# Three query tiles of an attention and gated-convolution kernel cast before they are turned, turned by the DMA engines instead of TensorE, under a newly searched order

## The chip, the core and the metric

The kernel runs on one core of a Trainium2 chip. The metric is the device time of the program in microseconds (us), as the median of several runs. Before the change it is 183.54 us (three runs, 183.1 to 183.88). One execution was taken by the hardware profiler; all durations below are from that one.

## What is computed

Inputs are q, k, v of 4 batches x 8 heads x 768 positions x 64 channels and three weight arrays. Attention keeps, for each query, the 6 best of 24 chunks of 32 keys; the rank of a chunk is an upper bound of its scores, made from the smallest and the largest key of the chunk in each channel. The result goes through a gated unit whose gate is a causal convolution of 5 taps.

```python
k_min, k_max = k_chunks.min(axis=3), k_chunks.max(axis=3)        # 24 chunks of 32 keys
ub = np.sum(np.maximum(q * k_min, q * k_max), axis=-1)           # query x chunk, causal chunks only
top_chunks = np.argsort(ub, axis=-1)[..., -6:]
scores = np.where(selected & causal, (q @ k.T) / 8, -1e9)
attn_out = softmax(scores) @ v                                   # B, H, S, 64 -> x: B, S, 512
gate = sigmoid(causal_conv5(x, conv_w))
out = (gate * (x @ w_val)) @ w_out
```

## The kernel before, in words

The 32 heads are worked on as 16 pairs (p = 0 to 15), two heads side by side on the 128 partitions; four pairs make one batch b. Every operation has a name, and the table ORDER (line 114) lists all names in the order in which they are emitted. Each engine carries out its own operations strictly in that order, each one waiting by semaphores for what it needs. So an operation whose input is late holds up all that stands behind it on its engine. The number behind "=" in ORDER is the PSUM bank that the operation takes.

For one pair (function pair in build, lines 297 to 480):

- Lk, Lq, Lv load k, q, v (line 632 for k and q, 628 for v), issued by SyncE (SP). Pair 0 is loaded in two parts, Lq0.0 and Lq0.1.
- KT and QT turn k and q on TensorE (PE), in fp32, 3 blocks of 128x128 to each of two halves w (line 641). KE (ScalarE, line 648) takes k out of PSUM as fp16; KX (VectorE, line 654) takes the smallest and largest key of each chunk. QH (ScalarE, line 683) gives the high fp16 part of 16 q, and QL (VectorE, line 722) the rest that fp16 lost, for the 640 queries from 128 on.
- KB, KS (GpSimd, lines 664 to 679) make the sums and differences of the chunk ends; AH and AL (VectorE, lines 729 and 732) the absolute values RH, RL of the two parts of q.
- CF and BD (PE, line 766; for pair 0 instead BF, line 714, in fp32) sum the upper bounds in PSUM. T8 (VectorE, line 774) finds the 8 largest, CM (line 781) writes the mask NS. The mask is turned either by PE and VectorE (MT, line 791, and ME, line 795) or, for pairs 10 to 15, by a DMA transpose that SP issues (MD, line 797).
- S (PE, lines 809, 811, 814): for each of six score banks the products of keys and queries, and the mask added by a second matmul (line 814). E (ScalarE, line 818): exp of a bank into P, for each of the two heads. A (GpSimd, line 830): the causal triangle. AV (PE, line 839), RC and NR (VectorE, lines 845 and 849): the sum over values and its division.
- XT turns the result for the second part: by PE and VectorE (XT, line 871, and XTE, line 882), or for pairs 8 to 14 by a DMA transpose (line 863). XH (GpSimd) copies 4 columns across block edges.

For two pairs, CV (PE, line 903) is the convolution, 160 small matmuls in two halves CVp.0 and CVp.1, and TH (ScalarE, line 908) its tanh. For each batch VL (PE, line 918, 16 matmuls) makes x w_val, GV (VectorE, line 924) the gate's product, OU (PE, line 932) the last product, OE (ScalarE, line 940; a few on VectorE, 942) takes it out, ST (SP, line 945) stores it. In the last batch VL is in two halves, VL3.n and VL3.nz.

At the start PE runs 36 matmuls on zeros, F and G (line 950), between the first operations. All loads of k, q and v, all stores and all DMA transposes go through SP's one queue. There is no planner at run time.

## Time and profile before

| | before |
|---|---|
| runs | 183.1, 183.54, 183.88 us |
| the profiled execution | 182.86 us |
| its span, first to last instruction | 181.2 us |
| busy: TensorE, its weight loads | 175.2, 127.3 us |
| busy: ScalarE, VectorE, GpSimd | 140.4, 123.3, 109.1 us |
| granted TensorE clock, mean | 1.00 |

The profiled execution's own time is 182.86 us, of which 181.2 lie between its first and its last instruction. Busy times count an instruction from its start to its end. Matmuls overlap, so a PE that is busy 97% of the span may still have been waiting between issues; the chain of waits and the start times of single pieces tell more. In a timeline row stand the start in us, the duration in us, engine, line and operation, what it writes and reads, the number of instructions merged, and in brackets the idle time of the engine ahead of it.

### The profile page before, as it was taken

The page shows a single profiled execution, that of the slowest core. Times are in us where ns is not written, and L with a number is a line of the kernel's source. Part 1 is how long each engine was busy: PE and PEld are TensorE (multiplying, and loading weights), DVE is VectorE, ACT ScalarE, POOL GpSimd, SP SyncE. Part 2 cuts the span into 40 slices and gives each one's busy share as a digit, 9 for nine tenths or more (in the row PEclk, how much of TensorE's full clock was granted, in tenths as well). Part 3 has the DMA queues.
Part 4 walks back from the last instruction along what each step waited for, and adds up shares of the span by engine and source line. Part 5 has one row for each costly group of instructions (what it writes and reads, how often), then busy time and mean ns, then how long its engine had stood idle before and what let it go on. Part 6 is the DMA issues. An engine that isn't in the chain of part 4 may idle for free.

```text
span 181.2 us, 8892 instructions
## 1 busy us (share of the span) xinstructions
PE 175.2 (97%) x3714; PEld 127.3 (70%) x3714; DVE 123.3 (68%) x429; ACT 140.4 (78%) x320; POOL 109.1 (60%) x309
## 2 busy tenths in 40 slices
PE   7999999999999999999999999999999999999991
PEld 5896667868878687787866685687567678656541
DVE  0569999999999799998765679558925233611360
ACT  2279999999999999999897867595867979357032
POOL 6955898999999979899919633374551615000000
PEclk9999999999999999999999999999999999999999
DMA  5999999999999999980697995895226149337045
GB/s 99 224 220 215 213 201 236 213 211 227 210 222 190 219 191 189 183 175 10 135 164 150 207 206 117 176 95 149 43 47 103 60 117 231 96 108 289 7 183 222
DMA packets 89912, 29.68 MB, mean 164 GB/s; under 512 B 85387, under 2 KB 86667, under 8 KB 89872
## 3 DMA queue, kind: packets, MB, share of 16 engines
q1 hardware_dynamic: 88880, 28.06, 73.5%
q0 software_dynamic: 992, 1.06, 4.5%
q8 instruction: 29, 0.48, 1.2%
q14 instruction: 11, 0.09, 0.2%
HBM read 20.98 MB, written 6.29 MB: 151 GB/s over the span
## 4 chain that ended last, share of the span: by engine, by line
PE 91%; DVE 5%; issue 1%; POOL 0%; ACT 0%
PE ps L918 12%; PE ps L839 12%; PE ps L932 12%; PE ps L641 11%; PE ps L811 10%; PE ps L903 9%; PE ps L814 9%; PE ps L766 6%; PE ps L950 4%; DVE KK L654 2%; PE ps L871 2%; PE ps L791 2%; PE ps L809 2%; PE ps L714 1%; DVE ON L849 1%
## 5 line engine op out<-in xcount | busy, mean ns | idle before, releaser
L818 ACT ACTIVATE P<-ps 128x512 f16<-128x512 f32 (+1 forms) x192 | 90.2, 600 | 5.4 <-PE ps L814 4.8
L830 POOL TENSOR_SCALAR_AFFINE_SELECT P<-P 128x256 f16<-128x256 f16 (+1 forms) x128 | 43.1, 358 | 23.6 <-ACT P L818 21.9
L654 DVE TENSOR_REDUCE KK<-ps 128x12 f32<-128x384 f32 x64 | 32.8, 550 | 7.1 <-PE ps L641 6.5
L814 PE MATMUL ps<-QM,EM 64*128 64x512 f16 (+4 forms) x256 | 36.9, 290 | 0.2
L811 PE MATMUL ps<-QH,KE 64*128 64x512 f16 (+4 forms) x256 | 35.1, 291 | 0.0
L924 DVE SCALAR_TENSOR_TENSOR GV<-G,ps 128x384 f16<-128x384 f32 x32 | 16.4, 548 | 22.8 <-PE ps L918 22.1
L839 PEld LDWEIGHTS <-P 128*128 128x128 f16 x672 | 26.1, 98 | 6.3 <-issue 3.3
L839 PE MATMUL ps<-VA,P 128*128 128x65 f16 x672 | 30.3, 194 | 0.2 <-issue 0.2
L940 ACT ACTIVATE OSB<-ps 128x512 f32<-128x512 f32 (+1 forms) x22 | 12.9, 594 | 15.6 <-PE ps L932 8.4
L918 PE MATMUL ps<-xT,wv 64*128 64x384 f16 x256 | 23.3, 323 | 0.3 <-issue 0.3
L932 PE MATMUL ps<-wo,GV 128*128 128x512 f16 (+1 forms) x100 | 22.7, 370 | 0.0
L774 DVE MAX8 TOP<-ps 128x8 f32<-128x16 f32 (+4 forms) x160 | 15.9, 166 | 6.6 <-PE ps L766 5.1
L918 PEld LDWEIGHTS <-wv 64*128 64x128 f16 x256 | 13.1, 94 | 8.3 <-issue 1.2
L908 ACT ACTIVATE G<-ps 128x384 f32<-128x384 f32 x32 | 13.9, 498 | 6.6 <-PE ps L903 6.6
L811 PEld LDWEIGHTS <-KE 64*128 64x128 f16 x256 | 13.6, 94 | 6.2 <-issue 1.6
L849 DVE TENSOR_TENSOR ON<-ps,RCP 128x384 f16<-128x384 f32 x32 | 17.5, 552 | 0.7
L648 ACT ACTIVATE KE<-ps 128x384 f16<-128x384 f32 x32 | 17.0, 569 | 1.0 <-DVE RCP L845 0.7
L683 ACT ACTIVATE QH<-ps 128x384 f16<-128x384 f32 x32 | 16.0, 556 | 2.3 <-PE ps L641 2.2
L903 PE MATMUL ps<-xT,diag 32*32 32x384 f16 x1280 | 17.3, 326 | 0.0
L741 POOL CAST VA<-vn 128x768 f16<-128x768 f32 x16 | 14.6, 915 | 3.8 <-DMA vn<-in_v_dram 3.7
L641 PE MATMUL ps<-ident,kn 128*128 128x128 f32 x96 | 15.7, 284 | 0.0
L903 PEld LDWEIGHTS <-diag 32*32 32x32 f16 x1280 | 14.0, 87 | 2.5 <-ACT P L818 0.4
(75 smaller groups left out, 304.3 us busy)
## 6 DMA issues: line engine op xcount, KB each, us to landing
vn<-in_v_dram SPq DMA_DIRECT2D x16, 384.0 KB, 6.1
out_dram<-OSB SPq DMA_DIRECT2D x23, 256.0 KB, 2.9
kn<-in_k_dram SPq DMA_DIRECT2D x30, 192.0 KB, 5.0
qn<-in_q_dram SPq DMA_DIRECT2D x30, 192.0 KB, 4.8
wv<-in_moe_w_val_dram POOLq DMA_DIRECT2D x8, 64.0 KB, 4.5
wo<-in_moe_w_out_dram POOLq DMA_DIRECT2D x4, 128.0 KB, 5.3
wv<-wv SPq DMA_DIRECT2D x4, 128.0 KB, 5.1
qn<-in_q_dram SPq DMA_DIRECT2D x4, 96.0 KB, 3.1
```

The lines of the kernel that those rows point to most:

```text
L641: nc.tensor.transpose(out=pt[:, tl * 128:(tl + 1) * 128], in_=t[:, 3 * w + tl, :], identity=ident)
L648: nc.scalar.activation(out=KE[p % 3][:, w * HB:(w + 1) * HB], in_=bank(gr, None), func=AF.Copy)
L654: nc.vector.tensor_reduce(out=KK[p % 2][:, mx, w * 12:(w + 1) * 12], in_=bank(gr, None).rearrange("p (c t) -> p c t", t=CH), axis=AX.X, op ...
L811: nc.tensor.matmul(out=pq[hh][:, col + a:col + n], lhsT=KE[p % 3][HP[hh], ks], rhs=QH[p % 3][HP[hh], q0 + a:q0 + n], start=True, stop=False)
L814: nc.tensor.matmul(out=pq[hh][:, col + a:col + n], lhsT=EM[HP[hh], ks], rhs=qm[HP[hh], q0 + a - 128:q0 + n - 128], start=False, stop=True)
L818: e.EX = lambda p, hh, bi, tot, gr: nc.scalar.activation(out=PT[hh, bi, p % 2][:, 0:tot], in_=bank(gr, None)[:, 0:tot], func=AF.Exp, scale ...
L830: nc.gpsimd.affine_select(out=ap, in_=ap, pattern=[[0, n], [1, 128]], compare_op=ALU.is_ge, fill=0.0, base=0, channel_multiplier=-1)
L839: nc.tensor.matmul(out=pav[:, qt, :], lhsT=PT[a, bi, p % 2][:, col:col + 128], rhs=VA[p % 3][:, hh, jt, :], start=(jt == 0), stop=(jt == qt))
L849: e.NR = lambda p, hh, gr: nc.vector.tensor_tensor(out=ON[(p // 2) % 2][:, 2 * (p % 2) + hh].rearrange("p t h d -> p h t d"), in0=bank(gr, ...
L903: nc.tensor.matmul(out=pc[i][os], lhsT=diag[rs, cp * NG + gi, j, :], rhs=x[rs, gi, :, a:a + 128], start=(j == 0), stop=(j == 2 * KSZ - 1), ...
L918: nc.tensor.matmul(out=pv[h], lhsT=wval_sb[HP[h], n, wc:wc + 255:2], rhs=xT[HP[h], (b % 2) * 2 + cp, gi, :, LD:LD + 128], start=(n == 0), ...
L932: nc.tensor.matmul(out=po[:, 0:z - a], lhsT=GVT[(b % 2) * NCT + et][:, s * 128:(s + 1) * 128], rhs=wout_sb[:, et, a:z], start=(et == 0), s ...
```

## The change

For pairs 13, 14 and 15 the operations QT, QH and QL go. In their place QN.0 (ScalarE) casts the 768 loaded, unturned queries to the high fp16 part, QN.1 (VectorE) makes the low part of 640 of them, and two DMA transposes on SP, QD.0 and QD.1, write them turned into QH and QL. The fp16 buffer of QN shares one tile (CW, two halves by p % 2) with the convolution's weights, which are loaded at the start. All else of the computation stays. The whole of ORDER is another one; the operations are the same but for the ones named.

```diff
+    "dmaq": set(range(13, 16)),
...
-        for w in range(2):
+        if p in P["dmaq"]:
+            b2 = p % 2
+            c, l = act(S)
+            g.op("ACT", c, l, f"QN{p}.0", lambda: e.QN(p, 0), [("qn", k4, 0), ("qn", k4, 1), ("cwps",)],
+                 [("QN", b2, 0)], ())
+            c, l = dve(SELT * 128)
+            g.op("DVE", c, l, f"QN{p}.1", lambda: e.QN(p, 1),
+                 [("qn", k4, 0), ("qn", k4, 1), ("QN", b2, 0)], [("QN", b2, 1)], ())
+            g.op("SP", 1300, 1300, f"QD{p}.0", lambda: e.QD(p, 0), [("QN", b2, 0)],
+                 [("QH", k3, w) for w in range(2)], (), dma=700.0)
+            g.op("SP", 1250, 1250, f"QD{p}.1", lambda: e.QD(p, 1), [("QN", b2, 1)],
+                 [("QL", k2, w) for w in range(2)], (), dma=650.0)
+        for w in range(2) if p not in P["dmaq"] else ():
...
-    cwl = ct_([KSZ, 2 * NG, 64], FP, "cwl")
-    cwn = ct_([KSZ, 2 * NG, 2, 64], FP, "cwn")
+    CW = ct_([128, 1536], FP, "CW")
...
+    QNA = CW.bitcast(F16).rearrange("p (i x) -> p i x", i=2)
...
+    def QN(p, n):
+        hi, lo = QNA[:, p % 2, 0:S], QNA[:, p % 2, S:S + SELT * 128]
+        t = qn[p % 4]
+        if n == 0:
+            nc.scalar.activation(out=hi, in_=t.rearrange("p t d -> p (t d)"), func=AF.Copy, scale=QS)
+        else:
+            nc.vector.scalar_tensor_tensor(
+                out=lo, in0=t[:, 1:NT].rearrange("p t d -> p (t d)"), scalar=QS, in1=hi[:, 128:S],
+                op0=ALU.mult, op1=ALU.subtract)
...
+    def QD(p, n):
+        dst, src = (QL[p % 2], QNA[:, p % 2, S:S + SELT * 128]) if n else (QH[p % 3], QNA[:, p % 2, 0:S])
+        nc.sync.dma_start_transpose(out=dst.rearrange("p (t c) -> p t c", c=128), in_=src)
...
 ORDER = """
-mKF0 wval30 mfz F0=0 F1 F2 F3 F4 F5 mxT F6 F7 F8 ident identb mKB1 cfill identh mVA0 F9 F10 F11 F12
...
+mfz F0=0 F1 F2 F3 F4 F5 F6 F7 F8 F9 F10 F11 F12 F13 F14 ident F15 Lk0.0 Lk0.1 mKF0 wval30 mxT identb
```

The order moves instructions on every engine. Three places follow, before and after. In the names, qn2 is the loaded q of pair 2, kn1 the loaded k of pair 1, ps_5 PSUM bank 5, fz the zeros of the F and G matmuls; "x3" are three instructions alike.

On PE, near the program's start, before: the transposes of pair 1's k (KT1) and of the second half of pair 0's q (QT0.1), one G matmul, and the first of the five bound sums of pair 0 (BF, lines 706 and 714).

```order
L641 MATMUL ps_5_261<-ident_61,kn1_75 128x128 x3
L641 MATMUL ps_6_267<-ident_61,kn1_75 128x128 x3
L641 MATMUL ps_7_279<-ident_61,qn0_78 128x128 x3
L950 LDWEIGHTS fz_145
L950 MATMUL ps_1_212<-fz_145 128x256
L706 LDWEIGHTS identb_65
L706 MATMUL ps_0_284<-cfill_64,identb_65 128x48
L714 MATMUL ps_0_284<-KF_105,QF_106 128x48 x2
```

The transposes of pair 2's q (QT2.1 and QT2.0) stand behind the fifth BF here.

The same place after the change, from QT0.1 (now line 655) to the first BF (now lines 720 and 728).

```order
L655 MATMUL ps_7_255<-ident_61,qn0_77 128x128 x3
L982 LDWEIGHTS fz_144
L982 MATMUL ps_1_221<-fz_144 128x256
L655 MATMUL ps_5_264<-ident_61,kn1_74 128x128 x3
...
L655 MATMUL ps_6_273<-ident_61,kn1_74 128x128 x3
...
L655 MATMUL ps_2_289<-ident_61,qn2_79 128x128 x3
L655 MATMUL ps_4_294<-ident_61,qn2_79 128x128 x3
L720 LDWEIGHTS identb_65
L720 MATMUL ps_0_299<-cfill_64,identb_65 128x48
L728 MATMUL ps_0_299<-KF_104,QF_105 128x48 x2
```

QT0.1 now stands ahead of both KT1, and both QT2 stand ahead of the five BF instead of behind them. Ahead of this piece 10 G matmuls stand in a row.

On VectorE, a little later, before: the end of the weights' split (cws), the mask of pair 0 taken out of PSUM (ME0, line 795) and what follows it.

```order
L1047 CAST cw2_71<-cwT_70 128x40
L1048 TENSOR_TENSOR cw2_71<-cwT_70,cw2_71 128x40
L795 COPY QM0_89<-ps_0_358 128x640
L722 SCALAR_TENSOR_TENSOR QL0_99<-ps_4_312,QH2_98 128x256
L722 SCALAR_TENSOR_TENSOR QL1_100<-ps_6_354,QH1_97 128x256
```

After the change, the same place.

```order
L1079 CAST cw2_70<-cwT_69 128x40
L1080 TENSOR_TENSOR cw2_70<-cwT_69,cw2_70 128x40
L743 TENSOR_SCALAR RH1_101<-QH1_96 128x640
L827 COPY QM0_88<-ps_0_365 128x640
L736 SCALAR_TENSOR_TENSOR QL0_98<-ps_4_294,QH2_97 128x256
```

AH1 (RH1, now line 743) has moved ahead of ME0.

On SP, in the second half, before: from the loads of pair 14 (kn2, qn2) to the mask transpose MD12 (QM0) and the next transposes and loads.

```order
L632 DMA kn2_76<-in_k_dram 128x6x64 x2
L632 DMA qn2_80<-in_q_dram 128x6x64 x2
L628 DMA vn0_82<-in_v_dram 128x12x64
L628 DMA vn3_85<-in_v_dram 128x12x64
L632 DMA kn3_77<-in_k_dram 128x6x64 x2
L632 DMA qn3_81<-in_q_dram 128x6x64 x2
L863 DMA_TRANSPOSE xT_73<-ON0_149 128x6x128
L945 DMA out_0_dram<-OSB3_170 128x512
L797 DMA_TRANSPOSE QM0_89<-NS0_119 128x5x128
```

After the change, the same stretch of SP's queue.

```order
L646 DMA kn2_75<-in_k_dram 128x6x64 x2
L764 DMA_TRANSPOSE QH1_96<-CW_68 128x6x128
L646 DMA qn2_79<-in_q_dram 128x6x64 x2
L642 DMA vn0_81<-in_v_dram 128x12x64
L646 DMA kn3_76<-in_k_dram 128x6x64 x2
L895 DMA_TRANSPOSE xT_72<-ON0_148 128x6x128
L764 DMA_TRANSPOSE QL1_99<-CW_68 128x5x128
L764 DMA_TRANSPOSE QH2_97<-CW_68 128x6x128
L829 DMA_TRANSPOSE QM0_88<-NS0_118 128x5x128
L764 DMA_TRANSPOSE QL0_98<-CW_68 128x5x128
L646 DMA qn3_80<-in_q_dram 128x6x64 x2
```

Four of the six QD (line 764) have come in between; pair 15's q is now loaded behind them and behind MD12 (line 829), and pair 15's v later still.

## The prediction

> **What bounds the kernel now.** I read the page first: the span, the busy times and the chain that ended last.

> ```profile
> span 181.2 us, 8892 instructions
> PE 175.2 (97%) x3714; PEld 127.3 (70%) x3714; DVE 123.3 (68%) x429; ACT 140.4 (78%) x320; POOL 109.1 (60%) x309
> PE 91%; DVE 5%; issue 1%; POOL 0%; ACT 0%
> ```

> The chain lies on PE for 91% of the span. But 78% for ACT is a mean over stages, so the busy times by stage come next (columns: PE, its weight loads, DVE, ACT, POOL, granted clock, DMA).

> ```profile
> 15.80:60.00 44.20, 43.78 (x787) 32.63 (x788) 42.92 (x162) 44.14 (x105) 39.09 (x110) 1.00 1.13 213
> 60.00:98.00 38.00, 37.72 (x1065) 29.24 (x1067) 32.33 (x110) 35.37 (x81) 30.75 (x84) 1.00 0.79 153
> 98.00:165.50 67.50, 67.50 (x1658) 47.15 (x1656) 34.75 (x115) 48.84 (x108) 27.30 (x84) 1.00 0.61 135
> 165.50:171.30 5.80, 5.48 (x69) 3.21 (x66) 1.57 (x3) 1.64 (x4) 0.00 (x0) 1.00 0.25 91
> ```

> The reader should see two regimes. From 15.8 to 60 us ACT works 44.14 of 44.20 us: the stage lasts as long as its exps and copies, from the first exp on. From 98 to 165.5 us PE works without a gap and ACT only 48.84 of 67.5. Between them both are nearly full (37.72 and 35.37 of 38). So work taken off PE after 98 us shortens the span at its full price, and a later first exp moves all that follows.

> **What goes.** The three changed pairs have their q transposes here, as merged pieces of the chain:

> ```profile
> 106.23 1.97 PE ps L641 x18
> 121.11 1.35 PE ps L641 x12
> ```

> The first piece holds QT13 and QT14 (12 transposes) beside KT14 (6), the second QT15 (6) beside KT15. One costs 1.97/18 = 0.109 us and 1.35/12 = 0.1125 us, so 12 x 0.109 + 6 x 0.1125 = 1.98 us of PE go, all where PE has no gap: **-1.98 us**.

> ACT and DVE give and take work in the same stage:

> ```profile
> L683 ACT ACTIVATE QH<-ps 128x384 f16<-128x384 f32 x32 | 16.0, 556 | 2.3 <-PE ps L641 2.2
> L722 DVE SCALAR_TENSOR_TENSOR QL<-ps,QH 128x256 f16<-128x256 f32 (+1 forms) x30 | 13.8, 480 | 0.7 <-ACT QH L683 0.4
> ```

> Six QH go (6 x 0.556 = 3.3 us); three QN.0 of 768 columns come, no row has that shape, and each costs between one QH and two (0.56 to 1.11). Six QL go (6 x 0.48 = 2.9 us); three QN.1 come, between one QL and two (0.48 to 0.96). Neither engine gets more work, and ACT has 67.5 - 48.84 = 18.7 us free there, DVE 32.75: nothing on the path. If that cover were gone the worst would be nothing still, since removed and added work are equal at the upper bounds.

> **What comes on SP.** Six DMA transposes, like those that are there:

> ```profile
> L797 SPq DMA_TRANSPOSE QM<-NS x6: 1201/1251/2170, 85.9 to 137.3; - x6
> DMA to landing us min/median/max: 2.5/2.6/3.5
> L863 SPq DMA_TRANSPOSE xT<-ON x7: 1242/1392/4467, 106.5 to 155.8; - x7
> DMA to landing us min/median/max: 2.7/3.6/7.5
> ```

> Each holds SP's queue 1.2 to 1.4 us and lands 2.6 to 3.6 us after issue; the slowest took 4.47 and 7.5. The place that counts is MD12, the mask transpose for which the first S12 waits on PE:

> ```profile
> 111.30 1.20 SPq L797 DMA_TRANSPOSE QM<-NS  x1
> 115.23 0.23 PE L811 MATMUL ps<-QH,KE 64*128 64x128 f16 x2
> ```

> Landing 2.6 us after 111.30 is 113.9; PE comes at 115.23, so 1.3 us are spare. Now QD13.1 and QD14.0 stand ahead of MD12 (2 x 1.25 = 2.5 us), but Lv15 and Lq15 have left that place, so SP arrives no later. I take 0 to 0.4 us for all new waits of this kind, **+0.2**, since the transposes nearest in kind (L797) spread little; the upper end is a rival. Behind QN13.0 and QN14.0 on ACT stand TH3 and the last E11, behind QN15.0 E12.10 and KE15; a wait there for a load falls into ACT's 18.7 free us. AL14 on DVE waits for QD14.1, and behind it stands GV1.2, whose bank PE needs only at VL1.0, three S12 later.

> **What is moved at the start.** Here the new order does something that has nothing to do with q's transposes. The chain to the first exp before:

> ```profile
> 8.77 0.82 PE L641 MATMUL ps<-ident,kn 128*128 128x128 f32 x6
> 9.63 0.52 PE L641 MATMUL ps<-ident,qn 128*128 128x128 f32 x3
> 10.13 0.62 PE L714 MATMUL ps<-KF,QF 128*128 128x48 f32 x4
> 12.54 0.84 PE L641 MATMUL ps<-ident,qn 128*128 128x128 f32 x6
> 12.74 0.92 DVE L774 MAX8 TOP<-ps 128x8 f32<-128x24 f32 x10 [1.50 <-PE ps L714]
> 14.81 0.49 DVE L795 COPY QM<-ps 128x640 f16<-128x640 f16 x1
> 15.80 1.08 ACT L818 ACTIVATE P<-ps 128x512 f16<-128x512 f32 x2 [0.16 <-PE ps L814]
> 16.81 0.32 DVE L729 TENSOR_SCALAR RH<-QH 128x640 uint16<-128x640 uint16 x1
> ```

> BF (L714) runs from 10.13 to 12.54, T8 waits for its end, and the mask (L795) and the first exp (15.80) follow. The loads that PE waits for, by issue on SP and time to landing:

> ```profile
> 5.88 0.49 SPq L632 DMA_DIRECT2D qn<-in_q_dram  x1
> qn<-in_q_dram SPq DMA_DIRECT2D x1, 96.0 KB, 3.6
> 6.94 0.89 SPq L632 DMA_DIRECT2D qn<-in_q_dram  x1
> qn<-in_q_dram SPq DMA_DIRECT2D x1, 192.0 KB, 4.3
> ```

> The second part of q0 lands at 5.88 + 3.6 = 9.5, q2 at 6.94 + 4.3 = 11.25. In SP's queue both keep their place (loads of the same sizes stand ahead). In the new order PE must do QT0.1, both KT1 and both QT2 before the first BF. QT0.1 starts at about 9.6, as before; KT1 and four zeros' matmuls follow until about 10.9 (the first piece's six took 0.82 for twice three, the zeros 0.11 each, by the piece quoted last); QT2 must wait for 11.25 plus the 0.15 us between landing and start that QT0.1 shows, and takes 6 x 0.11 = 0.66. BF starts at 12.05 instead of 10.13: 1.9 us later. AH1 now stands ahead of ME0 on DVE: 0.32 by the row at 16.81. The first exp comes 1.9 + 0.32 = 2.2 us later. ACT has the same operations before it (KE, QF, KF, QH of pairs 0 to 2) and can draw none forward, so the whole full stage of ACT moves: **+2.2 us**. Bounds: 0 if the loads land 2 us sooner, 2.6 if DVE's pieces stand less tightly. I take 2.2, since landings and order are both fixed.

> **Near the end** PE waits once in the last batch's VL:

> ```profile
> 98.21 1.30 PE ps L918 x16
> 165.54 3.03 PE ps L918 x36
> 168.57 0.32 issue
> 168.89 2.45 PE ps L918 x28
> ```

> Its 64 matmuls and the gap take 5.80 us; at 1.30 for 16 they would take 5.20. VL3.0 now comes first, in banks that CV13 and an OU leave, instead of VL3.1, which waits for TH15. I take **-0.4** of the possible 0.6 (0 if TH15 or GV3 is late in its place). CV13's two halves stand apart now. What an interruption costs is seen on CV3 and a whole one:

> ```profile
> 95.35 1.01 PE ps L903 x69
> 96.38 1.29 PE ps L903 x91
> 158.01 1.98 PE ps L903 x160
> ```

> 2.30 against 1.98: **+0.2**, between 0 and 0.3. The other switches between S and full-array work differ by a few and are not priced.

> **The sum** against the profiled execution's span: -1.98 + 0.2 + 2.2 - 0.4 + 0.2 = +0.2 us, from 181.2 to 181.4. That execution took 182.86 us in all, 1.7 outside its span; the median of the runs is 0.7 above it, and I add the sum to the median: 183.54 + 0.2 = 183.7 us. What a measurement of this kernel can tell from no change is about 0.5%, 0.92 us.

> [...] First the row:

> ```profile
> 1.22 4.88 PE ps L950 x22
> 7.73 1.20 PE ps L950 x11
> ```

> The same zeros' matmul takes 0.222 us at first and 0.109 later: PE ran at half rate until about 7 us, and never again in this trace. In the new order PE idles from about 8.4 (the end of its 10 G in a row, an estimate with 0.222 until 7 us and 0.11 after) to 9.6 and again 0.3 us before QT2, and from 8.4 to 12 us does little but transposes. [...]

> **The rivals.**

> *The late start costs nothing* (faster). If the loads land sooner, or the stage from 60 to 98 us takes up the delay (ACT is idle there 38 - 35.37 = 2.6 us), the 2.2 go: 183.7 - 2.2 = 181.5. For it: both engines are a little below full there. Against: PE is at 37.72 of 38, so ACT's idle time is waiting for PE, and a delay of both is not taken up. It decides if the first BF starts before 10.5 us. Chance 0.30.

> *MD12 is late* (slower). One of the two QD ahead of it in SP's queue is issued as slowly as the slowest L863 row, 4.47 instead of 1.25: 3.2 us, less the 1.3 spare, 1.9 us of PE waiting at the first S12, where PE has no gap: 183.7 + 1.9 = 185.6. For it: the slow issue stood behind two loads of v, and loads stand before QD13.1 too. Against: DMAs are at 0.61 in this stage. It decides when MD12 is issued less than 2.6 us before PE reaches S12. Chance 0.15.

> *PE falls back to half rate at the start* (slower). The five BF, 12.54 - 10.13 = 2.4 us, take twice that: 183.7 + 2.4 = 186.1. Chance 0.07.

> *The transposes go but PE gains nothing*, because another engine bounds the stage from 98 us: ACT at 48.84 of 67.5 and DVE at 34.75 speak against it; time 185.7. Chance 0.03.

> **How the numbers follow.** The forecast, start and transposes cancelling, has 0.45, its own range 182.8 to 184.9 by the bounds of its terms with the start at 1.9 to 2.6 (-1.98 + 1.9 - 0.6 = -0.7; -1.98 + 2.6 + 0.3 + 0.4 = +1.3). Faster by over 0.5% means under 182.6: the first rival (0.28 of 0.30, the rest partly taken up) and 0.04 of the forecast, 0.32. Slower, over 184.5: the three slower rivals 0.25 and 0.05 of the forecast, 0.30. The rest, 0.38, is no change. The range for 8 in 10 runs from 181.2, the first rival with 0.3 more from the end, to 186.0, which holds the MD12 case.

> **What would show it.** In the changed kernel's profile: L655 on qn with 18 matmuls fewer; the first BF (L728) at about 12.0 and the first exp (L850) at about 18.0; ACT without idle from there to about 62; CV1's piece of 160 some 2.2 us later; the first VL of batch 3 without the 0.3 us gap; QM's first matmul of pair 12 without a wait. The prediction is wrong if the first exp comes at 16 or sooner, if ACT has gaps before 60 us, if PE waits for QM, QH or QL after 98 us, or if PE's matmuls at 10 to 14 us take twice their time.

## The result, and the profile after

The changed kernel takes 185.82 us (median; 185.52 to 187.34) against 183.36 us for the kernel before on the same chip: a ratio of 1.0128, 95% interval 1.0081 to 1.0176. It is slower by about 2.4 us. The forecast of no change (183.7 us, a sum of +0.2 us) was 2.1 us too low. That the time lies in the range given is luck: the upper end of that range stood for a late MD12, and MD12 was not late. The profiled execution took 185.98 us with a span of 184.3 us, 3.1 more than before. All ratios here are formed from undisturbed runs; the one profile that fell into a disturbed run (e7) is not read.

First the page of the kernel after: the span, the busy times and the chain that ended last.

```profile
span 184.3 us, 8878 instructions
PE 174.2 (95%) x3696; PEld 124.7 (68%) x3696; DVE 123.6 (67%) x426; ACT 140.5 (76%) x317; POOL 110.8 (60%) x309
PE 67%; POOL 12%; DVE 11%; SPq 3%; DMA 2%; ACT 2%; issue 2%; ACTq 0%; POOLq 0%; DVEq 0%
```

TensorE has its 18 instructions and 1.0 us of work less, and the span is longer all the same. The chain tells where to look: it lay on PE for 91% and does so for 67% now, with GpSimd (12%), which had nothing of it before, and VectorE in its place. What TensorE waited for, kernel before, then kernel after (total, times, longest, in us; the wait for fz is the program's start in both):

```profile
PE ps L950 <- DVE fz L963: 1.2, 1, 1.2
PE ps L918 <- issue: 0.3, 1, 0.3
PE ps L839 <- issue: 0.2, 1, 0.2
PE ps L791 <- DVE NS L781: 0.2, 1, 0.2
```

```profile
PE ps L655 <- DMA qn<-in_q_dram: 1.2, 2, 1.0
PE ps L982 <- DVE fz L995: 1.1, 1, 1.1
PE ps L871 <- POOL P L862: 0.9, 2, 0.5
PE ps L846 <- DVE QM L827: 0.8, 2, 0.5
PE ps L950 <- DVE GV L956: 0.6, 1, 0.6
PE ps L823 <- DVE NS L813: 0.6, 2, 0.4
PE ps L871 <- DVE QL L736: 0.5, 1, 0.5
PE ps L798 <- POOL KB L688: 0.3, 1, 0.3
```

In waits of over 0.15 us, the ones listed, TensorE lost 0.7 us behind its first matmul before and 4.9 us after. Three places are to be seen: the start (qn, NS, QM), the middle (P, KB, QL), the last part (GV).

The start, kernel after, PE, then ACT's first exp:

```profile
9.30 0.52 PE L655 MATMUL ps<-ident,qn 128*128 128x128 f32 x3 [0.96 <-DMA qn<-in_q_dram]
11.19 0.84 PE L655 MATMUL ps<-ident,qn 128*128 128x128 f32 x6 [0.27 <-DMA qn<-in_q_dram]
17.73 1.08 ACT L850 ACTIVATE P<-ps 128x512 f16<-128x512 f32 x2 [1.23 <-PE ps L846]
```

The first exp comes at 17.73 instead of 15.80: +1.93 us. Next the starts of CV1 and CV5, kernel before and kernel after:

```profile
60.39 2.10 PE L903 MATMUL ps<-xT,diag 32*32 32x384 f16 x160
85.89 0.99 PE L903 MATMUL ps<-xT,diag 32*32 32x384 f16 x34
```

```profile
62.63 2.18 PE L935 MATMUL ps<-xT,diag 32*32 32x384 f16 x160
89.96 1.34 PE L935 MATMUL ps<-xT,diag 32*32 32x384 f16 x96
```

CV1 is 2.24 us late, as the start has it. CV5 is 4.07 us late: another 1.83 us have gone between them. A row of GpSimd of the kernel after shows where:

```profile
60.22 0.89 POOL L773 CAST VA<-vn 128x768 f16<-128x768 f32 x1 [1.96 <-DMA vn<-in_v_dram]
```

The cast of v5 (VC5) waits 1.96 us for its load. From 67.88 to 85.13 us the chain of the kernel after then lies on GpSimd without a break: it does not catch up before CV5.

The stages, columns as in the prediction (length, PE, its weight loads, DVE, ACT, POOL, clock, DMA), cut at the first exp, CV1, the first VL of batch 0, and the first VL of batch 3; kernel before, then after:

```profile
15.80:60.39 44.59, 44.17 (x789) 32.86 (x789) 43.31 (x163) 44.53 (x105) 39.48 (x110) 1.00 1.12 213
60.39:98.05 37.66, 37.38 (x1063) 29.02 (x1064) 31.94 (x109) 35.03 (x81) 30.41 (x84) 1.00 0.79 152
98.05:165.47 67.42, 67.42 (x1657) 47.12 (x1654) 34.75 (x115) 48.78 (x108) 27.25 (x84) 1.00 0.61 135
165.47:181.20 15.73, 11.71 (x104) 6.25 (x96) 5.80 (x11) 4.41 (x9) 0.00 (x0) 1.00 0.40 151
```

```profile
17.73:62.63 44.90, 44.17 (x790) 32.80 (x790) 42.32 (x162) 44.72 (x106) 36.70 (x103) 1.00 1.06 201
62.63:102.06 39.43, 37.73 (x1065) 29.12 (x1065) 33.01 (x110) 35.70 (x82) 34.79 (x96) 1.00 0.83 150
102.06:168.93 66.87, 66.21 (x1639) 44.72 (x1636) 34.84 (x112) 47.22 (x101) 27.28 (x81) 1.00 0.75 142
168.93:184.30 15.37, 11.53 (x104) 6.13 (x96) 5.71 (x11) 5.27 (x12) 0.00 (x0) 1.00 0.50 189
```

Row by row: +1.93 to the first exp, +0.31, +1.77, -0.55, -0.36: together +3.10 us. GpSimd's work has moved into the second of these stages: it did 39.48 us of work in the first stage before and 36.70 after, and 34.79 instead of 30.41 in the second. The third stage, where 1.98 us of transposes left TensorE, is only 0.55 us shorter.

### The profile page after: what moved, and what is told of

Read it like the earlier page. It is cut to its first block, busy times and chain, and to the rows that moved or that the text cites. A ratio compares the mean times of both kernels' runs of the same rounds, so it can differ in the third digit from the quotient of the medians.

```text
span 184.3 us, 8878 instructions
## 1 busy us (share of the span) xinstructions
PE 174.2 (95%) x3696; PEld 124.7 (68%) x3696; DVE 123.6 (67%) x426; ACT 140.5 (76%) x317; POOL 110.8 (60%) x309
## 4 chain that ended last, share of the span: by engine, by line
PE 67%; POOL 12%; DVE 11%; SPq 3%; DMA 2%; ACT 2%; issue 2%; ACTq 0%; POOLq 0%; DVEq 0%
PE ps L950 12%; PE ps L964 11%; PE ps L871 9%; PE ps L935 8%; PE ps L843 7%; PE ps L846 6%; PE ps L655 6%; POOL P L862 5%; PE ps L798 4%; SPq L646 3%; DVE KK L668 2%; DMA qn<-in_q_dram 2%; DVE TOP L806 2%; DVE RH L743 2%; DVE QL L736 1%
## 5 line engine op out<-in xcount | busy, mean ns | idle before, releaser
L850 ACT ACTIVATE P<-ps 128x512 f16<-128x512 f32 (+1 forms) x192 | 89.9, 573 | 6.6 <-PE ps L846 6.1
L862 POOL TENSOR_SCALAR_AFFINE_SELECT P<-P 128x128 f16<-128x128 f16 (+1 forms) x128 | 44.8, 373 | 26.8 <-ACT P L850 25.4
L846 PE MATMUL ps<-QM,EM 64*128 64x512 f16 (+4 forms) x256 | 36.0, 290 | 0.8 <-DVE QM L827 0.8
L843 PE MATMUL ps<-QH,KE 64*128 64x512 f16 (+4 forms) x256 | 33.9, 291 | 0.0
L950 PE MATMUL ps<-xT,wv 64*128 64x384 f16 x256 | 23.1, 323 | 0.6 <-DVE GV L956 0.6
L806 DVE MAX8 TOP<-ps 128x8 f32<-128x24 f32 (+4 forms) x160 | 15.8, 165 | 4.8 <-PE ps L798 2.5
L662 ACT ACTIVATE KE<-ps 128x384 f16<-128x384 f32 x32 | 16.5, 554 | 3.2 <-PE ps L655 2.4
L950 PEld LDWEIGHTS <-wv 64*128 64x128 f16 x256 | 13.0, 94 | 8.5 <-issue 1.3
L655 PE MATMUL ps<-ident,kn 128*128 128x128 f32 x96 | 16.5, 291 | 0.0
L964 PEld LDWEIGHTS <-GV 128*128 128x128 f16 x100 | 9.1, 98 | 9.7 <-issue 0.9
## 6 DMA issues: line engine op xcount, KB each, us to landing
out_dram<-OSB SPq DMA_DIRECT2D x23, 256.0 KB, 3.3
kn<-in_k_dram SPq DMA_DIRECT2D x30, 192.0 KB, 5.3
qn<-in_q_dram SPq DMA_DIRECT2D x30, 192.0 KB, 4.9
```

Of the source, the lines that this page charges most:

```text
L655: nc.tensor.transpose(out=pt[:, tl * 128:(tl + 1) * 128], in_=t[:, 3 * w + tl, :], identity=ident)
L806: nc.vector.max(out=TOP[p % 2][:, it - 1, s, :], in_=bounds(gr)[:, it - 1, s * NCH:s * NCH + n])
L843: nc.tensor.matmul(out=pq[hh][:, col + a:col + n], lhsT=KE[p % 3][HP[hh], ks], rhs=QH[p % 3][HP[hh], q0 + a:q0 + n], start=True, stop=False)
L846: nc.tensor.matmul(out=pq[hh][:, col + a:col + n], lhsT=EM[HP[hh], ks], rhs=qm[HP[hh], q0 + a - 128:q0 + n - 128], start=False, stop=True)
L850: e.EX = lambda p, hh, bi, tot, gr: nc.scalar.activation(out=PT[hh, bi, p % 2][:, 0:tot], in_=bank(gr, None)[:, 0:tot], func=AF.Exp, scale ...
L862: nc.gpsimd.affine_select(out=ap, in_=ap, pattern=[[0, n], [1, 128]], compare_op=ALU.is_ge, fill=0.0, base=0, channel_multiplier=-1)
```

## The experiments

Ratios are to the kernel before, run on the same chip in turn with the experiment. First exp, CV1 and CV5 are starts in the profile (us); "PE idle" is the sum of the idle time ahead of TensorE's matmuls behind the first one.

| run | ratio, 95% interval | span | first exp | CV1 | CV5 | PE idle |
|---|---|---|---|---|---|---|
| before | 1 | 181.2 | 15.80 | 60.39 | 85.89 | 1.1 |
| after | 1.0128 [1.0081, 1.0176] | 184.3 | 17.73 | 62.63 | 89.96 | 5.1 |
| e1 | 1.0187 [1.0140, 1.0233] | 183.8 | 16.24 | 62.59 | 88.67 | 5.6 |
| e2 | 1.0140 [1.0093, 1.0187] | 183.1 | 17.81 | 62.69 | 88.94 | 4.6 |
| e3 | 1.0399 [1.0342, 1.0455] | 188.8 | 17.79 | 62.66 | 89.62 | 7.8 |
| e4 | 1.0150 [1.0110, 1.0190] | 184.6 | 19.08 | 63.89 | 89.41 | 2.0 |
| e5 | 1.0828 [1.0762, 1.0893] | 194.4 | 17.84 | 62.41 | 87.91 | 13.5 |
| e6 | 1.0133 [1.0085, 1.0182] | 184.7 | 16.02 | 61.54 | 89.40 | 6.2 |
| e7 | 1.0124 [1.0063, 1.0185] | | | | | |
| e8 | 1.0148 [1.0104, 1.0192] | 184.3 | 18.41 | 63.32 | 88.83 | 2.8 |
| e9 | 1.0746 [1.0688, 1.0804] | 195.7 | 15.61 | 60.19 | 86.41 | 13.0 |
| e10 | 1.0074 [1.0041, 1.0107] | 183.1 | 16.08 | 61.61 | 87.88 | 3.9 |
| e11 | 1.0129 [1.0079, 1.0179] | 182.8 | 15.62 | 60.26 | 85.77 | 4.1 |
| e12 | 1.0099 [1.0039, 1.0158] | 183.8 | 15.54 | 60.18 | 86.32 | 4.9 |

My theory after the result: the loss is the late start (about 2 us) and GpSimd's wait for v5 (1.8 us), less what the transposes are worth. The rival: the loss lies in the DMA transposes themselves.

### The start: e1, e4, e8

e1 puts the start of the new order back:

```diff
-QT0.1=7
...
-QH0.1
...
 KT1.1=6
+QT0.1=7 QF0.1 RF0.1 QH0.1
...
-QF0.1 RF0.1
...
-QT2.1=2
...
-QT2.0=4
...
 BF0.5
+QT2.1=2 QT2.0=4
...
+ME0
 AH1
-ME0
```

> The changed kernel with the start put back: both QT2 behind the five BF, QT0.1 behind KT1 and AH1 behind ME0 as before the change, and QH0.1 behind RF0.1; the rest of the new order and the DMA transposes stay. Theory A (the late start carries through one to one): the first BF at about 10.2 us and the first exp at about 16, 1.7 to 2.0 us sooner, and the time 185.8 - 1.9 = 183.9 us; GpSimd's wait of 1.96 us for v of pair 5 stays, since loads and GpSimd move together. If that wait is only a consequence of the late start, it goes too and the time is 182.0. Rival B (the start is absorbed later, the new order loses its time elsewhere): the first exp is sooner, the time stays at 185.8.

The first exp came 1.5 us sooner, and nothing of it was left at CV1: 62.59 against 62.63. The next wait stood close behind. PE in e1:

```profile
19.49 0.52 PE L655 MATMUL ps<-ident,kn 128*128 128x128 f32 x3 [0.85 <-DMA kn<-in_k_dram]
```

The new order has a transpose of k3 (KT3.0) early, ahead of S0.0. With the late start its load was there in time; with the earlier one TensorE waits for it, and ScalarE behind it. So theory A fell for this order, and so did the sum made with it: the ratio of e1 (1.0187) is no better than that of the changed kernel (1.0128).

e4 does the reverse, alone, in the order of before:

```diff
+Lq2.0 KE0.1 QT2.1=2 QT2.0=4
 BF0.2=0 BF0.1 cwl
-KE0.1
 RF0.1 QF0.1 BF0.5 BF0.3 BF0.4 em2 QH0.1
-Lq2.0 QT2.1=2 QT2.0=4
```

> The kernel before with only one place of its start changed: both QT2 ahead of the five BF instead of behind them, so that BF waits for the load of q2. Theory A (a late first exp carries through one to one): first BF at about 12.0 instead of 10.13, first exp at about 17.7, time 183.4 + 1.9 = 185.3 us. Rival B (the stage from 60 to 98 us takes it up): first exp late just the same, time 183.4 to 184.

The time rose by 1.5%, 2.75 us, more than theory A asked for. In the profiled execution the first exp came at 19.08 and not at 17.7. Two windows of e4 (length, PE, weight loads, DVE, ACT, POOL, clock, DMA) tell why:

```profile
13.00:16.00 3.00, 3.00 (x22) 2.91 (x21) 0.70 (x9) 0.25 (x1) 1.96 (x6) 0.54 1.39 220
16.00:19.00 3.00, 3.00 (x24) 2.00 (x24) 2.70 (x15) 0.98 (x2) 0.00 (x0) 0.50 1.26 210
```

The granted clock fell to one half at about 13.2 us (0.54 over three us is 0.24 us at 1.0 and the rest at 0.5). In the kernel after the first of these windows has the full clock:

```profile
13.00:16.00 3.00, 2.74 (x30) 2.48 (x28) 1.49 (x16) 1.35 (x5) 1.68 (x5) 1.00 1.39 220
```

PE's rows of e4 ahead of the fall:

```profile
9.24 0.52 PE L641 MATMUL ps<-ident,qn 128*128 128x128 f32 x3
9.60 0.27 PE L950 MATMUL ps<-fz 128*128 128x256 f16 x1
11.06 0.85 PE L641 MATMUL ps<-ident,qn 128*128 128x128 f32 x6 [1.19 <-DMA qn<-in_q_dram]
11.77 0.62 PE L714 MATMUL ps<-KF,QF 128*128 128x48 f32 x4
```

The last matmul on zeros ends at 9.87; behind it stand 1.19 us of waiting for q2, six transposes and, from 11.77, the fp32 bound sums. From 9.87 to 13.2 are 3.3 us, and the longest idle time in them is 1.19 us. The length of such a stretch alone does not decide. Between the last zeros' matmul and the first matmul of S, the kernel before has 4.8 us (10.26 to 15.04) and the kernel after 5.6 us (10.91 to 16.55) of transposes and small sums, the latter with waits of 0.27 and 0.35 us, and both keep their clock (1.00 from 9 to 16 us in both).

e8 is e4 with six zeros' matmuls moved in between, so that the clock might hold:

```diff
-G7 G4 G16
...
-G1
...
-G2
...
-G0
...
 Lq2.0 KE0.1
+G16 G1 G2 G0 G4 G7
 QT2.1=2 QT2.0=4
```

> As e4 (the kernel before with both QT2 ahead of the five BF), with six of the zeros' matmuls moved from ahead of KT1 to just ahead of QT2, so that TensorE has no single idle stretch of 1.2 us there. Theory A (in e4 the granted clock fell to half rate from 13 to 20 us because of that idle stretch, which made the start 1.4 us later still): the clock stays at 1.0, first exp at 17.7 instead of 19.1, CV1 at about 62.3, time 183.3 + 1.9 = 185.2 us. Rival B (a late start of 1.9 us is taken up before the end, and e4's 2.7 us were all the clock's): clock 1.0, first exp 17.7, time 183.3 to 183.9. Rival C (the clock falls all the same): first exp 19, time 186.

It went as rival C has it, only later: the clock was 0.53 from 16 to 19 us, the first exp came at 18.41, the ratio was 1.0148. The fall came 5.4 us behind the last zeros' matmul here (10.78 to 16.2).

A late start at full clock is on record too. e5, which stands further below for another reason, has the start of e4 operation for operation: the same one zeros' matmul (it ends at 10.26), 1.20 us of waiting ahead of QT2, the same sums behind. Its clock row reads 0.9 or more in every slice up to 131 us, and the last of its bound sums takes 0.62 us for four matmuls (14.12) where that of e4 took 1.07 (14.19). Its first exp, CV1 and CV5 came at 17.84, 62.41 and 87.91, which is 2.04, 2.02 and 2.02 us late. So the order alone does not make the clock fall, and the zeros' matmuls are not shown to hold it; the six runs of e4 list mean clocks from 0.979 to 1.000. What sets off the fall stays open. For the late start itself e5 is the clean case: to CV5 it carries through one to one, as theory A has it. For the whole time there are only e4 and e8, with the slower clock in them: first exps 3.28 and 2.61 us late, in the one execution of each that was profiled, and 2.75 and 2.7 us of time (183.4 x 0.0150 and 0.0148), 0.84 and 1.03 of their size.

### The middle: e2, e6, e10

e2 puts three operations of GpSimd ahead of VC5 in the new order:

```diff
 dg03
+dg10 dg12 wval11
...
 VC5 A5.05
-wval11
...
-dg12
...
-dg10
```

> The changed kernel with GpSimd's cast of v of pair 5 (VC5) behind three operations that wait for nothing (wval11, dg12, dg10, together about 2.06 us) instead of ahead of them. Theory A (GpSimd is without slack from 58 to 85 us, so its wait of 1.96 us for that load moves all behind it): the wait goes, the convolution of pair 5 (CV5) starts 1.5 to 1.9 us sooner, time 185.8 - 1.8 = 184.0 us. Rival B (GpSimd's wait hides behind ScalarE, TensorE or the late loads): the wait goes but CV5 moves by less than 0.4 us and the time stays at 185.8.

In the profile the wait was gone, though VC5 itself started as late as ever (60.20 against 60.22); CV5 came 1.02 us sooner (88.94), and the span was 1.2 us shorter. In the times it does not show: 1.0140 against 1.0128, with intervals of 0.9%. By itself e2 is inconclusive.

e6 is e2 with the start of e1 and KT3.0 later, so that k3 need not be there yet:

```diff
-KT3.0=3
 dg02 Lk4.0 Lv0 E0.03 S0.0=45
...
 BD1.3
+KT3.0=3
 A0.13
```

> The changed kernel with the start of e1, KT3.0 moved from ahead of S0.0 to behind BD1.3 on TensorE (so that it no longer waits 0.85 us for the load of k3), and GpSimd's cast of v5 behind three operations as in e2. Theory A (in e1 the 1.5 us won at the start were lost again on this one load and then on ScalarE's idle 1.8 us behind it): first exp 16.2, no wait of TensorE for kn, CV1 at 60.9 to 61.4 instead of 62.6, time 185.8 - 1.3 (e1's start) - 1.2 (e2) = 183.3 us. Rival B (the loads as a whole hold the stage from 16 to 60 us, and another load takes its place): first exp at 16.2, CV1 still at 62.2 to 62.7, time 184.8 to 185.5.

CV1 starts at 61.54, so 1.09 of the 1.71 us from the start arrived there, but CV5 only starts at 89.40, and the ratio (1.0133) is that of the changed kernel, as rival B has it. GpSimd's row of VC5 in e6:

```profile
60.86 0.87 POOL L773 CAST VA<-vn 128x768 f16<-128x768 f32 x1 [1.82 <-DMA vn<-in_v_dram]
```

With three operations more ahead of it VC5 waits as long as ever: GpSimd comes sooner, the load does not. What sets the time there is when v5 lands. Rival B was right that another load takes the place, and it is one that can be named. SP loads v7 ahead of v5, as it did before; but before, GpSimd cast v7 first (58.39 us, v5 at 60.80), and in the new order it casts v5 first. e10 is e6 with the two loads the other way round:

```diff
-Lq8.0 Lv7 Lv5
+Lq8.0 Lv5 Lv7
```

> As e6, and SP loads v5 ahead of v7 instead of behind it (the new order has GpSimd take v5 first, and v7 lands 1.5 us ahead of it). Theory A (e6 kept GpSimd's wait of 1.8 us because this one load lands at 60.7 whatever stands ahead of it on GpSimd): GpSimd's wait for v5 falls under 0.5 us, CV5 at 88.0 to 88.6 instead of 89.4, time 185.2 - 1.2 = 184.0 us. Rival B (GpSimd or the stage behind it is the bound in its own right, the wait was only its place): the wait goes, CV5 within 0.4 us of e6's 89.4, time 185.2.

VC5 in e10 stands right behind the work ahead of it:

```profile
59.12 0.88 POOL L773 CAST VA<-vn 128x768 f16<-128x768 f32 x1
```

No idle time stands in its row, CV5 starts at 87.88 instead of 89.40, and the ratio falls from 1.0133 (e6) to 1.0074 [1.0041, 1.0107]. For the wait and for CV5 theory A holds: one load, one place late in SP's queue, cost 1.5 us at CV5. In the time it is about 1.1 us (0.0059 x 183.8), but the two intervals overlap, and with their widths the difference is known to about 0.0058: it is only just clear of the noise. e10 is the fastest form of the new order; the kernel before is still faster. Against the changed kernel the mends of start and load together gave about 1.0 us (1.0128 to 1.0074), where my theory had 3.8.

### The transposes: e3, e5, e9, e11, e12

e3 keeps the new order and has TensorE turn the queries of pairs 13 to 15 again (QT13 behind XT8, QT14 behind XTE7, QT15 behind KT15 and CM13).

> The new order, but the queries of pairs 13 to 15 turned on TensorE again (QT, QH, QL put in beside KT14 and KT15; no QN, no QD). Theory A (TensorE is the bound after 98 us, the 18 transposes cost 1.98 us there): 185.8 + 2.0 = 187.8 us, or 187.0 if the waits of VectorE for QL by DMA (3.16 and 0.6 us) now cost up to 0.8 us of it. Rival B (the DMA transposes give back all that they save, by these waits): 185.8 within 0.5. Rival C (they cost more than they save, and the slowdown is theirs): 183.5 to 185.

It took 2.7% more than the changed kernel, about 5 us, more than the 2.0 that theory A gave. The rest is waiting, after 98 us:

```profile
PE ps L965 <- DVE QL L737: 2.4, 2, 1.7
```

OU waits for a bank that VectorE has not read out. The places of the QT were chosen by hand, so e3 does not price the transposes; it shows only that the new order without them is no better, which speaks against the rival that the DMA transposes are the loss.

The other way round, the order of before with only the transposes taken off, should show their worth: e5, e9 and e11. e5 also kept the late start of e4, by oversight.

> The order of before, with only the 18 transposes of pairs 13 to 15 taken off TensorE: QT, QH, QL of these pairs go, QN and QD come at their places; Lk15, Lq15 and the first store move behind MD12 on SP, and AL14 behind GV1.0 on VectorE. The start and all else is as before. Theory A (TensorE is the bound after 98 us, so the transposes are worth their time when nothing new waits): the time falls by 1.98 us less at most 0.6 of waits, 183.3 - 1.4 to 2.0 = 181.3 to 181.9 us, with the start (first exp 15.8, CV1 60.4, CV5 85.9) unchanged. Rival B (the DMA transposes give back what they save): 183.3 within 0.5. Rival C (they cost more): over 184.

> What e5 was to be: the order of before, its start untouched, with only the transposes of pairs 13 to 15 taken off TensorE. (e5's order held e4's late start by an oversight, and its AH14 on VectorE stood ahead of T8 and CM of pair 12 and waited 4.4 us for QH by DMA.) Here QD14.0 and QD14.1 stand behind MD12 on SP, AL13 behind NR10.1, AH14 and AL14 behind GV1.0, QN15.1 behind four of T8 of pair 13, AH15 behind GV1.3 on VectorE, so that nothing that VectorE does for pair 12 or batch 1 stands behind a wait for a DMA transpose. Theory A (TensorE is the bound after 98 us and the transposes are worth their time where nothing waits for a DMA): first exp 15.8, CV1 60.4, VL of batch 0 at 98 as before, TensorE idle under 2 us in all, time 183.4 - 1.98 + (0 to 0.6) = 181.4 to 182.0 us. Rival B (each DMA transpose gives its gain back in a wait somewhere): 183.4 within 0.5, with TensorE's idle time up by about 2 us. Rival C: over 184.

e9's change against before, without the removals and without the moves that the expectation names:

```diff
 E10.12
+QN13.0
...
 Lk14.0
+QD13.0
...
 GV0.21
+QN13.1 QD13.1
...
 KX14.01
+QN14.0 QN14.1
...
 CM12 MD12
+QD14.0 QD14.1
...
 E12.03
+QN15.0 QD15.0
...
 T813.4
+QN15.1 QD15.1
```

e5 and e9 took 8.3% and 7.5% more, far over theories A and B; rival C (over 184) has the direction, and had named no size. SP's rows of e9:

```profile
100.61 1.17 SPq L646 DMA_DIRECT2D qn<-in_q_dram  x2
105.95 1.20 SPq L764 DMA_TRANSPOSE QL<-CW  x1
...
115.87 2.47 SPq L829 DMA_TRANSPOSE QM<-NS  x1
```

SP stood from 101.8 to 105.95 us because QD13.1 waited for VectorE's cast; four loads, XT8 and MD12 stood behind it, MD12 went at 115.87 instead of 111.30, and TensorE waited 3.65 us for its mask. For the mask of MD13, which stood behind QD15.0 and QD15.1, it waited 4.33 us more:

```profile
PE ps L846 <- DMA QM<-NS: 8.0, 2, 4.3
```

This is the prediction's rival with MD12 (1.9 us there), behind another transpose, about twice as large, and a second time with MD13. e11 moves four of the six transposes in SP's queue and nothing else (QD13.0 behind Lv15, QD13.1 behind Lq15.0, QD15.0 and QD15.1 behind MD13).

> As e9, with the DMA transposes put elsewhere in SP's queue: QD13.0 behind the load of v15 and QD13.1 behind the load of q15 (in e9 SP stood still from 101.8 to 105.95 us because QD13.1 waited for VectorE's QN13.1, and the loads, XT8 and MD12 behind it came 4.6 us later), QD15.0 and QD15.1 behind MD13. Theory A (e9's 13 us were head-of-line waits in SP's queue and not the price of the transposes): MD12 is issued at 111 to 112 as before, TensorE does not wait for QM, and the time is 183.6 - 1.98 + (0 to 0.6) = 181.6 to 182.2 us. Rival B (the transposes themselves, or the casts, hold ScalarE, VectorE or SP up wherever they stand): TensorE waits elsewhere for as long, 183.5 or more.

The ratio fell from 1.0746 to 1.0129 and MD12 went at 109.98: the 11 us were the queue. 8.0 of them are the two waits themselves; behind these waits the granted clock of e9 fell as well (0.73 from 120 to 126 us, 0.89 from 130 to 145). Theory A was right about the queue. But its time was not had: e11 is not faster than before, although TensorE has 18 matmuls less and starts as early. What it waited for after 98 us:

```profile
PE ps L935 <- issue: 1.6, 1, 1.6
PE ps L798 <- DVE TOP L806: 1.1, 1, 1.1
PE ps L787 <- ACT P L850: 0.4, 1, 0.4
PE ps L964 <- ACT P L850: 0.3, 1, 0.3
```

The 1.1, 0.4 and 0.3 us (1.10, 0.45 and 0.31) are where the QT had stood. Before, TensorE turned q while T8 was under way; without the transposes it waits 1.10 us for it: it had no gap there because they filled it. The other two have a second reason. By the order they stand ahead of CF14 and OU0.2 (the expectation of e12 calls them CF13 and OU0.5), which wait for the last exps of pair 12, and ScalarE takes these behind the new cast QN15.0, which lasts 0.85 us. So 1.86 of the 1.98 us come back as waiting. The first row is of another kind:

```profile
158.07 1.83 PE L935 MATMUL ps<-xT,diag 32*32 32x384 f16 x137
161.47 0.51 PE L935 MATMUL ps<-xT,diag 32*32 32x384 f16 x23 [1.57 <-issue]
```

Within CV13 TensorE stands 1.57 us for nothing that the profile names. e12 is e11 with CV13 behind the OU and OE that follow it, so that the same place of the stream falls into other work, and with T812.5 drawn ahead and QN15 later, against the waits for TOP and P:

```diff
 T812.3
+T812.5
...
-T812.5
...
-QN15.0
...
 E12.01
+QN15.0
 T813.1 T813.5
...
-QN15.1
...
 CM13
+QN15.1
 MD13 QD15.0
...
 XT15=3 XTE15
-CV13.0=0217 CV13.1 TH13.01
 OU2.4=5 OE2.4
-XH15
 OU1.3=6 OE1.3 OU2.3=3 OE2.3
+OU1.4=4 OE1.4 CV13.0=0217 CV13.1 TH13.01 XH15
...
-OU1.4=4 OE1.4
```

> As e11, with each of the waits of TensorE that e11's profile shows after 98 us addressed by a move. (1) T8 12.5 directly behind T8 12.3 on VectorE: in e11 TensorE's BD12.1 waited 1.10 us for it. (2) QN15.0 behind the last exp of pair 12 on ScalarE and QN15.1 behind CM13: in e11 CF13 and OU0.5 waited 0.45 and 0.31 us for banks that an exp behind QN15.0 was to free. (3) The four OU (2.4, 1.3, 2.3, 1.4) with their OE ahead of CV13 instead of behind it. In e5, e9 and e11 TensorE stood 1.86, 1.92 and 1.57 us inside CV13 for nothing that the profile names, each time ahead of the same instruction of its stream (number 6849 or 6850, counting weight loads); all other such gaps over 0.2 us of these runs stand at numbers that differ from it by a multiple of 256 or nearly so. Theory A (TensorE's code comes in blocks of 256 instructions, and one block was not there in time because CV eats 320 in 2 us): with the slow OU ahead of CV13 the same block is asked for earlier, and the gap falls under 0.5 us. Theory A for the whole: all three waits go, time 184.0 (the kernel before) + 1.6 (e11's span over before's) - 1.1 - 0.75 - 1.3 = 182.5 us. Rival B for the gap (something of CV13 itself, its diag or its banks, is late): the gap stays at 1.5 us before the same matmul of CV13. Rival C for the rest (each wait taken away opens another): time within 0.5 of before, 183.5 to 184.5, with TensorE's idle time near 3 us.

CV13 ran through. The gap was now in CV15:

```profile
163.95 1.28 PE L935 MATMUL ps<-xT,diag 32*32 32x384 f16 x89 [0.57 <-ACT G L940]
167.43 1.09 PE L935 MATMUL ps<-xT,diag 32*32 32x384 f16 x71 [2.21 <-issue]
```

That is ahead of instruction 7105 of TensorE's stream: 6849 + 256. Rival B for the gap (something of CV13) is out; the gap belongs to the place in the stream, as theory A has it, though its size did not fall as theory A said; CV13 and CV15 now follow each other, and the block that was late lies wholly within the two (more on this in the last section). As for the rest, rival C was nearer: the wait of BD12 fell from 1.10 to 0, and one of 0.77 for GV opened behind it; the ratio is 1.0099, about 185.5 us, above even rival C's time. No version beat the kernel before.

e7 is e6 with AL14 behind GV1.00 on VectorE:

```diff
-AL14 GV1.21 E12.02 S12.4=61 E12.14 VL1.0=20 GV1.20 E12.04 S12.1=53 E12.01 GV1.00
+GV1.21 E12.02 S12.4=61 E12.14 VL1.0=20 GV1.20 E12.04 S12.1=53 E12.01 GV1.00 AL14
```

> As e6, and VectorE's AL14 (which waits 3.1 us for the QL of pair 14 that comes by DMA) behind GV1.00 instead of ahead of the GV1 pieces. Theory A (VectorE waiting in its place holds up GV1.2 and with it the banks of VL1.0): TensorE's idle time from 105 to 135 us falls by 0.5 to 0.8 us, time 0.5 to 0.8 us under e6. Rival B (the wait is hidden, TensorE has other work): same as e6 within 0.3.

1.0124 against e6's 1.0133, each known to about 0.005: the 0.5 to 0.8 us of theory A, 0.3 to 0.4%, would not show here, so e7 decides nothing.

## Why the prediction was wrong, point by point

**The start: right in mechanism and size.** BF at 12.05 was forecast, 11.90 measured; first exp at 18.0 and 17.73; CV1 +2.2 and +2.24. That the last two agree so closely is partly luck: the first exp was 1.93 late, and 0.31 came in the stage behind it. e5 shows the carry of a late start to CV5 one to one, so the rival by which it costs nothing is out. The five BF took 2.41 us (11.90 to 14.31), as before (10.13 to 12.54), at a granted clock of 1.00, so the rival at half rate did not come; that the clock can fall in such a start e4 (0.54 from 13 to 16 us) and e8 (0.53 from 16 to 19 us) show. The granted clock also reads 1.00 while the kernel before's first zeros' matmuls take 0.222 us each (1.22 to 6.10 us); what makes these slow was not shown.

**60 to 98 us: the term that was missing, and the largest error.** The prediction said that both engines are nearly full there and gave the stage no price. It cost 1.77 us. It had read TensorE and ScalarE, and SP's loads only at the start and around MD12. That GpSimd takes v5 ahead of v7 while SP loads v7 first is told by the order; in the trace it is 1.96 us of waiting. e10 against e6 shows the wait gone and CV5 1.5 us sooner, with a gain in time only just clear of the noise. None of the signs by which the prediction was to be known wrong came up: they, too, were all on TensorE, ScalarE and the start.

**-1.98 for the transposes: the step that failed.** "All where PE has no gap" was taken to mean full price. The stage got 0.55 us shorter. 0.66 us came back as waiting (66.87 - 66.21), nearly all of it TensorE's wait for GV that is the next point, the other 0.77 as busy time: PE's fell by 67.42 - 66.21 = 1.21 and not by 1.98. The stage has the same matmuls less 18 (1657 and 1639), so the others took longer: CV13's halves by 0.22, the rest is not traced to single pieces. e11 shows another side of it in the order of before: 1.86 us of waiting where the transposes had been, 1.10 of them for a T8 that the transposes had covered. An engine without gaps is not an engine whose every piece is on the path.

**AL14: wrong by 0.6 us.** I priced its wait for QD14.1 at nothing, since the bank is wanted three S12 later. VectorE in the kernel after:

```profile
120.36 0.55 DVE L746 SCALAR_TENSOR_TENSOR RL<-QH,QL 128x320 uint32<-128x320 uint32 x1 [3.16 <-DMA QL<-CW]
```

QD14.1 was issued behind MD12, at 115.96, and landed 4.4 us later, where the prediction had taken 2.6 to 3.6 from other transposes. GV1.2 stands behind AL14, and VL1.0 waits 0.64 us. Whether moving it gains anything e7 did not show.

**MD12: right for the change.** SP issued it at 114.66 us and TensorE did not wait for the mask. That the mechanism is real, and can cost 11 us, e9 and e11 show.

**The end: right.** The gap in VL is gone and the stage is 0.36 us shorter, against -0.4; CV13's halves take 1.10 + 1.10 us against 1.98, +0.2 as forecast. Rows of the chain after:

```profile
157.88 1.10 PE ps L935 x80
162.01 1.10 PE ps L935 x80
168.99 5.31 PE ps L950 x64
```

The sum was +0.2 us; with 1.77 us more in the middle and 1.03 less of a gain after 98 us (-1.98 + 0.2 + 0.2 = -1.58 forecast for that stage, -0.55 measured) it is +3.0, against 3.1 measured in the span. What stays open: how much of the new order's loss is in the order as a whole. e10 mends the load and part of the start (CV1 at 61.61) and still has 0.7% over the kernel before, and no version here has both that kernel's flow and the gain of the transposes.

## What to carry to other kernels

Work taken off an engine that is busy all the time need not shorten its stage by as much: here 1.98 us off TensorE gave 0.55. Before pricing it, look at what is released within the time of the removed piece, since the engine may wait for that (1.10 us for a T8 in e11). Where an order is replaced, compare for every queue the order of the loads with the order in which they are used; one pair that changed places cost 1.5 us at CV5 and about 1 us of time here. A DMA that waited for a cast held up all of SP's queue from 101.8 to 105.95 us in e9: put such a DMA behind everything that could go without it.

## What the hardware showed that I had not expected

A CV has 320 instructions in 2 us, so each CV holds at least one border of a block; with one border none of the CVs of the kernel before stands still. The long ones came where a whole block of 256 lay in such a run and was used up in 1.8 to 2.6 us: without the 18 matmuls the borders at 6593 and 6849 both lie inside CV13, and in e12 those at 6849 and 7105 lie inside CV13 and CV15. The code's own packets agree. The page of the kernel before has this queue (packets, MB, share):

```profile
q8 instruction: 29, 0.48, 1.2%
```

That is one packet of 16 KB for about every 256 of TensorE's 7484 instructions: from the end of the first of the 29 packets to the end of the last TensorE starts 255.8 instructions per packet, in the kernel after 256.0. Each of the sixteen idle times ends 1.31 to 1.62 us behind the end of such a packet; in e11 it took from 158.55 to 160.08, and TensorE went on at 161.47. At all but 16 of the 377 borders (29 in each of the thirteen profiles) no such idle time of over 0.15 us stands; at the 16 it is up to 2.21 us.

The granted clock fell to one half in a start of transposes and small fp32 sums whose longest idle time was 1.19 us (e4, at 13.2 us; 0.50 from 16 to 19 us), and did not in an execution of the same start in e5 (0.9 or more up to 131 us). Behind waits of 3.65 and 4.33 us it fell as well (e9, 0.73 from 120 to 126 us and 0.89 from 130 to 145). A single profile at full clock does not show that a start is safe from the fall: the mean clocks of e4's six runs go from 0.979 to 1.000.
